# One attention pass for the first batch, a first chunk of 512 tokens, and a new split of the weight decode between ScalarE, VectorE and GpSimd

## The chip, the core and the metric

The kernel runs on one core of a Trainium2 chip. The core has five engines that each work through their own list of instructions in order: TensorE (PE in the profile; its weight loads are PEld), VectorE (DVE), ScalarE (ACT), GpSimd (POOL) and SyncE (SP), which here does nothing but issue the DMA transfers. The metric is the time of one execution in microseconds. The kernel before has a median of 1164.68 us over three runs, from 1161.99 to 1166.79.

## What is computed

A causal attention with a cumulative bias is followed by two gated feed-forward stages. Shapes: 4 batches, 8 heads, 576 positions, head size 64, so 2304 tokens of width 512; the first stage has 1536 hidden columns, the second 2048. The weights arrive as float64.

```python
scores = scale * np.matmul(q, k.transpose(0, 1, 3, 2))
cum = np.cumsum(np.maximum(s, 0.0), axis=-1)
bias = -(cum[:, :, :, None] - cum[:, :, None, :])
scores = np.where(causal, -1000000000.0, scores + np.minimum(bias, 0.0))
attn = np.exp(scores - np.max(scores, axis=-1, keepdims=True))
attn = attn / (np.sum(attn, axis=-1, keepdims=True) + 1e-09)
x = np.matmul(attn, v)           # heads side by side: 2304 x 512
x = (x @ w_a) * (x @ w_b) @ moe_w_out
h = x @ w_in
out = (np.maximum(h, 0.0) ** 2) @ moe2_w_out
```

## The kernel before

**Recording and planning.** Nothing is issued where it is written. Each operation is recorded with the engines that may do it and a cost for each. `Plan.order` (line 145) then goes through a simulated clock: for each engine it takes the operation that can start first, with a rank by stream (`RANK`, line 77) to choose between those that are ready, and so fixes both the engine and the place of every instruction. A buffer tag has a number of buffers; an operation that needs a new one waits until an older tile of the tag has had its last use. Costs are written by hand: `on_dve`, `on_act`, `on_gps` (lines 323 to 330) and `dma` (line 341), which counts 3.0 ns per kilobyte. Operations marked as using a port that VectorE and GpSimd share are kept apart in the plan. `copy` may go to ScalarE or VectorE, `subtract` to GpSimd or VectorE. Nearly every instruction carries line 246 in the profile, the line in `Plan.run` that issues it, so groups are told apart by tile names.

**Attention.** `attention` (line 723) works on pairs of heads. For a head, `softmax` (line 570) makes the scores (`st`) bank by bank: the products, then a product with a constant `mask` that adds the causal -1e9, then the row maximum on VectorE (`neg`), the exponential on ScalarE (`e`, with the row sum as a second output), a reciprocal (`one`) and the scaling of `e` by whichever of three engines is free. `weigh` (line 662) transposes `e` (`pt`), copies it (`ph`, and a remainder `pl`) and multiplies by the values (`av`), giving `u`. Batch 0 uses plain float32 operands (`fq`, `fk`, where the cumulative sum rides as a 65th row); batches 1 to 3 use split operands (high part and remainder) made by `prep` (line 531) from `raw` tiles.

**The first batch in two passes.** Before, batch 0 is done in a pass over queries 0 to 255 (stream "first", keys 0 to 255 alone) and later in a pass over queries 256 to 575 (stream "att").

**First stage.** `moe1` (line 852) goes over chunks of tokens: 256, 320, and four of 432. For each of 12 slices f of the hidden columns, 24 products of 128x128 weights with the chunk's columns make `ab` (two groups of 12), VectorE and ScalarE multiply and split the result, and after every third f 36 products `py` add to the output. A chunk is thus 432 products: 36 groups of 12. A chunk needs all heads of its tokens. Chunk 0 takes its input straight from `u`; others read it back from DRAM (`xd`).

**Weights.** `split_w` (line 815) decodes the three float64 matrices, 36 tiles of 128x512, on the chip: `decode` (line 780) loads 512 KB, scales the high word as a float and converts the low word with a scale (the two *scales*), shifts and merges the bits (two VectorE instructions), adds on GpSimd, casts to the high part `wh` on ScalarE and *subtracts* for the remainder (`wl`, `wlo`), which is also stored to DRAM (`wlab`, `wlo`) for the later chunks. The raw words land in `roomxh`, `roomxl` and, for the first `MORE` tiles, `words`. Chunk 0 runs f by f as the tiles appear. The second stage's weights are decoded the same way by `split2` (line 981) late in the first stage.

**Around the start.** `ssb`, `spos`, `ch`, `cl`, `maskf` and the q and k tiles of batches 1 to 3 share the tag `raw` (three buffers). `ch` and `cl`, the two parts of the cumulative sum, are stored to DRAM as `cd` when `operands` (line 492) is first called, which is in the preparation of batch 1. `maskf` is filled on GpSimd and cast to `mask` on ScalarE.

Of the kernel before, what the change touches and what calls it, by code (L numbers as in the profile page):

```python
# [7 lines left out]
F32 = mybir.dt.float32  # L8
# [8 lines left out]
P = 128  # L17
# [231 lines left out]
def attention_moe_moe(tc, q, k, v, s, w_a, w_b, w_out, w_in2, w_out2, out):  # L249
# [11 lines left out]
    CA = 256  # L261
    CB = S - CA
    GRP = 3
    GB = 4
    NT1 = 3
    CC = 432
# [6 lines left out]
    MORE = 24  # L273
# [49 lines left out]
    def on_dve(method, n, *args, two=False, each=1.04, **kw):  # L323
        return "DVE", 150 + each * n, two, method, args, kw
# [27 lines left out]
    def subtract(n, out, a, b, by="PD"):  # L352
# [10 lines left out]
        [scratch([NP, P, CB if b == 0 else S], F32, f"xd{b}")] for b in range(B)  # L363
    ]

    spans = [(0, CA), (CA, S)] + [(t, t + CC) for t in range(S, B * S, CC)]
# [14 lines left out]
    def blocks(q0, qn):  # L381

        if qn == S:
            return [(0, 64)] + [(64 + P * i, P) for i in range(4)], 0
        if q0 == 0:
            return [(0, P), (P, P)], 0
        return [(0, P), (P, P), (256, 64), (320, P), (448, P)], 2

    def load_values(b, p, q0, qn):

        t = at([P, NJ, P], F32, "val", 2, f"val{b}_{p}_{q0}")
        kb, _ = blocks(q0, qn)
# [20 lines left out]
    first_q = [at([P, S], F32, "T2q", 3, f"fq{i}") for i in range(3)]  # L413
    first_k = {}

    def load_first(hh, q0, qn):
        kn = q0 + qn
        tq = first_q[hh % 3]
        tk = first_k[hh, q0] = at([P, S], F32, "T2k", 3, f"fk{hh}_{q0}")
        dma(tk[:D, :kn].part("x"), k[0, hh, :, :kn], kn * 0.25)  # L420
        dma(tq[:D, :qn].part("x"), q[0, hh, :, q0 : q0 + qn], qn * 0.25)

    ssb = at([P, S], F32, "raw", 3, "ssb")[: B * H]
    dma(ssb, s.rearrange("b h s -> (b h) s"), 74)
    for hh in range(3):
        load_first(hh, 0, CA)

# [7 lines left out]
    spos = at([P, S], F32, "raw", 3, "spos")[: B * H]  # L435
# [5 lines left out]
    ch, cl = (at([P, S], F32R, "raw", 3, z)[: B * H] for z in ("ch", "cl"))  # L441
# [4 lines left out]
    maskf = at([P, S], F32, "raw", 3, "maskf")[:, :P]  # L446
# [8 lines left out]
    for i in range(4):  # L455
        t = [at_const([P, NJ + 2], F32, f"{z}{i}") for z in ("neg", "sum", "one")]
        for x in t:
            gps("memset", NJ + 2, x, 1.0)
        small.append(t)
# [3 lines left out]
    def score_banks(q0, qn):  # L463
        if qn == S:
            return [[(1, 0, 192), (2, 0, 320)], [(0, 0, 64), (3, 0, 448)], [(4, 0, 288)], [(4, 288, 288)]]
        if q0 == 0:
            return [[(0, 0, P), (1, 0, CA)]]
        return [[(2, 0, 320)], [(3, 0, 448)], [(4, 0, 288)], [(4, 288, 288)]]


    def weight_banks(q0, qn):
        if qn == S:
            return [(0, 320, [[0], [1, 2]]), (320, 256, [[1, 2], [3, 4], [0]])]
        if q0 == 0:
            return [(0, CA, [[0, 1]])]
        return [(256, 320, [[0, 4], [1], [3], [2]])]

    def load_pair(b, p, src, nm):
        t = at([P, S], F32, "raw", 3, f"raw{nm}")
        dma(t, src[b, 2 * p : 2 * p + 2].rearrange("h d s -> (h d) s"), 288)  # L480
        return t
# [26 lines left out]
    def prep_first(p, q0, qn):  # L508

        load_values(0, p, q0, qn)  # L510
        heads = []
        for hh in (2 * p, 2 * p + 1):
            if (hh, q0) not in first_k:
                load_first(hh, q0, qn)
            tk = first_k[hh, q0]
            dma(tk[D : D + 1, : q0 + qn].part("c"), cum[hh : hh + 1, : q0 + qn], 2)
            tq = first_q[hh % 3]
            scaled(qn, tq[:D, :qn].part("x"))
            heads.append((tq, tk))
        return heads  # L520
# [10 lines left out]
    def prep(b, p):  # L531
# [4 lines left out]
        load_values(b, p, 0, S)  # L536
        scaled(S, tq)
        heads = []
        for h in range(2):
            hh = b * H + 2 * p + h  # L540
            t1 = operands()
            t2q = at([P, S], F32R, "T2q", 3, f"t2q{nm}_{h}")
            t2k = at([P, S], F32R, "T2k", 3, f"t2k{nm}_{h}")
# [26 lines left out]
    def softmax(b, p, h, q0, qn, head):  # L570

        kb, first_block = blocks(q0, qn)
        banks = score_banks(q0, qn)
        nq = len(kb)
        nm = f"{b}_{p}_{q0}_{h}"
# [5 lines left out]
        for i, pieces in enumerate(banks):  # L581
            ps = mm_bank(f"st{nm}_{i}") if b == 0 and q0 == 0 and hh % 2 else bank(f"st{nm}_{i}")
# [5 lines left out]
            for blk, k0, kn in pieces:  # L588
                at_, m = kb[blk]
                qc = slice(at_ - q0, at_ - q0 + m)  # L590
# [44 lines left out]
            for blk, k0, m, to, kn, ee in held:  # L635
# [4 lines left out]
                    accum_out=tot[:m, c : c + 1].part(c), psum=True,  # L640
# [21 lines left out]
    def weigh(b, p, h, q0, qn, head, place, chunk, u):  # L662

        kb, first_block = blocks(q0, qn)
        g0, n, banks = chunk
        nm = f"{b}_{p}_{q0}_{h}_{g0}"
        parts = []
        for i, keys in enumerate(banks):
            ps = bank(f"pt{nm}_{i}", "t")
            calls, ins, off, spans = [], [ident], 0, []  # L670
            for j in keys:
                k0, m = kb[j]
                c0 = max(k0, g0)
                for blk in range(max(j, first_block), len(kb)):
# [434 lines left out]
```

## Time and profile before

The profiled execution is one of its own, outside the three runs.

| What | Value |
|---|---|
| median of three runs | 1164.68 us |
| profiled execution | 1163.58 us |
| its span, first to last instruction | 1161.8 us |
| granted TensorE clock, mean over the span | 0.964 |
| TensorE products | 5888 instructions recorded, 1105.1 us busy (95%) |
| VectorE | 1315 instructions, 670.9 us (58%) |
| ScalarE | 1164 instructions, 494.9 us (43%) |
| GpSimd | 284 instructions, 324.3 us (28%) |
| DMA | 143.85 MB, mean 124 GB/s |
| first and last product with chunk 0 | 46.2 and 239.7 us |
| first product of chunk 1 | 241.3 us |
| last product of batch 3's attention | 525.4 us |
| first product of the second stage | 752.0 us |

In the rows of the profile a tile's buffer number is left out: `ab<-xh,wh` is a product of a weight tile `wh` with a chunk's columns `xh`. Products overlap each other, so the time that one product is recorded with (350 ns for 432 columns) is longer than the time from one to the next; a group of 12 in the chain of waits gives the pace.

### The profile page before, as it was taken

The numbers are of one execution on the slowest core, as the hardware profiler recorded it, in microseconds if no ns is written. First come the engines' busy times: TensorE is split into PE (matmuls) and PEld (weight loads), VectorE is DVE, ScalarE is ACT, GpSimd is POOL, SyncE is SP. The second block draws the span as 40 slices with busy tenths as digits, with TensorE's granted clock in tenths as the row PEclk, the third lists the DMA queues.
The fourth block names the chain that finished last, engine by engine and source line by source line (L and its number), as shares of the span: only waits on it lengthen the run. The fifth ranks groups of instructions, "written<-read, shape, count | busy, mean of one in ns | idle before, by whom it ended". The sixth has DMA issues, their size and how long they took to land.

```text
span 1161.8 us, 16590 instructions
## 1 busy us (share of the span) xinstructions
PE 1105.1 (95%) x5888; PEld 969.6 (83%) x5888; DVE 670.9 (58%) x1315; ACT 494.9 (43%) x1164; POOL 324.3 (28%) x284
## 2 busy tenths in 40 slices
PE   5888987699999999999999999998999999999998
PEld 4666666599999999999999999987888888888887
DVE  6778988877888878863232257887232232232232
ACT  5567656557666665442121135455322222222222
POOL 3456655433433342210010036677100010000000
PEclk9689987799999999999999999999999999999999
DMA  6767575664456454335353387653020020010000
GB/s 186 221 187 237 184 219 156 192 175 149 151 170 178 137 158 116 115 100 154 113 164 124 101 271 239 195 175 124 1 73 1 1 73 1 1 55 1 1 37 19
DMA packets 91314, 143.85 MB, mean 124 GB/s; under 512 B 10320, under 2 KB 60240, under 8 KB 91232
## 3 DMA queue, kind: packets, MB, share of 16 engines
q1 hardware_dynamic: 91232, 142.80, 39.9%
q8 instruction: 46, 0.75, 0.3%
q14 instruction: 36, 0.29, 0.1%
HBM read 110.68 MB, written 23.22 MB: 115 GB/s over the span
## 4 chain that ended last, share of the span: by engine, by line
PE 83%; DVE 7%; DMA 5%; issue 1%; POOL 1%; ACT 1%; SPq 0%; DVEq 0%; POOLq 0%; ACTq 0%
PE ab L246 24%; PE po L246 16%; PE ph L246 16%; PE py L246 12%; PE st L246 6%; PE pt L246 5%; PE av L246 5%; DMA loo<-wlo 1%; DVE roomxl L246 1%; DVE neg L246 1%; DVE ph L246 1%; DMA lo<-wlab 1%; DVE one L246 1%; DMA roomxh<-in_moe_w_a 1%; DMA words<-in_moe_w_a 0%
## 5 line engine op out<-in xcount | busy, mean ns | idle before, releaser
L246 DVE SCALAR_TENSOR_TENSOR ph<-ph,r 128x512 f32<-128x512 f32 (+1 forms) x80 | 51.6, 645 | 198.7 <-ACT r L246 198.6
L246 ACT ACTIVATE r<-ph 128x512 f32<-128x512 f32 (+1 forms) x80 | 44.5, 556 | 221.5 <-PE ph L246 221.5
L246 PE MATMUL ab<-xh,wh 128*128 128x432 f32 (+1 forms) x384 | 134.4, 350 | 0.0
L246 PE MATMUL ab<-xl,wh 128*128 128x432 f32 (+1 forms) x384 | 132.7, 346 | 0.0
L246 PE MATMUL ab<-xh,lo 128*128 128x432 f32 (+1 forms) x384 | 132.7, 345 | 0.0
L246 PE MATMUL po<-w2h,g2h 128*128 128x512 f32 x288 | 113.0, 393 | 3.2 <-ACT g2h L246 3.1
L246 ACT ACTIVATE e<-st,neg 128x192 f32<-128x192 f32 (+4 forms) x192 | 92.3, 483 | 54.6 <-DVE neg L246 45.2
L246 PE MATMUL po<-w2l,g2h 128*128 128x512 f32 x288 | 113.0, 392 | 0.0
L246 PE MATMUL po<-w2h,g2l 128*128 128x512 f32 x288 | 112.7, 391 | 0.0
L246 DVE TENSOR_TENSOR ab<-ab,a 128x432 f32<-128x432 f32 (+2 forms) x72 | 40.7, 565 | 113.5 <-PE ab L246 109.4
L246 PE MATMUL pt<-ident,e 128*128 128x128 f32 (+3 forms) x480 | 89.3, 295 | 14.3 <-ACT e L246 5.7
L246 DVE TENSOR_REDUCE neg<-st 128x1 f32<-128x192 f32 (+4 forms) x192 | 79.0, 429 | 16.8 <-PE st L246 13.0
L246 PEld LDWEIGHTS pt<-ident,e 128*128 128x128 f32 (+3 forms) x480 | 57.0, 140 | 34.7 <-ACT e L246 7.6
L246 PE MATMUL py<-gh,wh 128*128 128x432 f32 (+1 forms) x240 | 85.0, 354 | 0.2 <-DVE gl L246 0.2
L246 PE MATMUL py<-gl,wh 128*128 128x432 f32 (+1 forms) x240 | 83.6, 348 | 0.0
L246 PE MATMUL py<-gh,loo 128*128 128x432 f32 (+1 forms) x240 | 83.5, 348 | 0.0
L246 DVE TENSOR_TENSOR g2l<-ph,g2h 128x512 fp32r<-128x512 f32 (+1 forms) x80 | 50.9, 638 | 44.1 <-ACT g2h L246 39.7
L246 ACT COPY a<-ab 128x432 f32<-128x432 f32 (+2 forms) x72 | 34.5, 480 | 93.2 <-PE ab L246 92.9
L246 PEld LDWEIGHTS ab<-xh,lo 128*128 128x128 f32 x384 | 72.2, 188 | 2.2
L246 PEld LDWEIGHTS ab<-xh,wh 128*128 128x128 f32 x384 | 72.4, 189 | 2.0
L246 PEld LDWEIGHTS ab<-xl,wh 128*128 128x128 f32 x384 | 72.4, 189 | 1.9
L246 PE MATMUL av<-ph,vs 128*128 128x320 f32 (+1 forms) x192 | 63.0, 330 | 5.6 <-DVE ph L246 4.7
(214 smaller groups left out, 2820.6 us busy)
## 6 DMA issues: line engine op xcount, KB each, us to landing
lo<-wlab SPq DMA_DIRECT2D x60, 512.0 KB
loo<-wlo SPq DMA_DIRECT2D x48, 384.0 KB
v_0r<-in_moe_w_in SPq DMA_DIRECT2D x16, 512.0 KB
v_1r<-in_moe_w_out SPq DMA_DIRECT2D x16, 512.0 KB
out<-o SPq DMA_DIRECT2D x18, 256.0 KB
roomxh<-in_moe_w_a SPq DMA_DIRECT2D x8, 512.0 KB
roomxh<-in_moe_w_b SPq DMA_DIRECT2D x8, 512.0 KB
roomxl<-in_moe_w_out SPq DMA_DIRECT2D x8, 512.0 KB
```

The costliest lines, as they stand in the source:

```text
L246: getattr(eng, method)(*map(real, args), **{k: real(a) for k, a in kw.items()})
```

## The change

Five things are changed together, and the planner then makes a new order of everything:

1. Batch 0's attention is one pass over all 576 queries, with the same banks as the other batches, all in stream "first". `FIRST` = 512 of its tokens go straight to chunk 0 (eight tiles `x0`), the last 64 to DRAM.
2. The chunks are 512 and four of 448, so five in place of six.
3. In `decode` both scales are done by ScalarE alone, for both stages' weights; the first stage's subtract is done by VectorE alone. The second stage's subtract stays on GpSimd.
4. Buffers are fewer: `raw`, `T2q`, `T2k` and `T1` have two in place of three, `ph` two in place of three, `MORE` is 20 in place of 24.
5. The planner counts 4.5 ns per kilobyte of DMA in place of 3.0, and counts VectorE's fast copies and scales as users of the port shared with GpSimd. The row sums get one reduction over three columns (two partial sums and 1e-9) in place of an addition of 1e-9 and, where there were two parts, a reduction of two.

```diff
-    CA = 256
-    CB = S - CA
+    FIRST = 512
-    NT1 = 3
-    CC = 432
+    NT1 = 2
+    CC = 448
-    MORE = 24
+    MORE = 20
...
-        return "DVE", 150 + each * n, two, method, args, kw
+        return "DVE", 150 + each * n, two or each < 1, method, args, kw
...
-        pl.call(("SP", kb * 3.0, False, "dma_start", (out, in_), {}), takes=takes, lag=lag)
+        pl.call(("SP", kb * 4.5, False, "dma_start", (out, in_), {}), takes=takes, lag=lag)
...
-    spans = [(0, CA), (CA, S)] + [(t, t + CC) for t in range(S, B * S, CC)]
+    spans = [(0, FIRST)] + [(t, t + CC) for t in range(FIRST, B * S, CC)]
...
-    ssb = at([P, S], F32, "raw", 3, "ssb")[: B * H]
+    ssb = at([P, S], F32, "raw", 2, "ssb")[: B * H]
...
-    maskf = at([P, S], F32, "raw", 3, "maskf")[:, :P]
+    maskf = at([P, S], F32, "raw", 2, "maskf")[:, :P]
...
-        if banks[-1][0][1]:
-            dve("tensor_reduce", 2, out=tot[:, nq - 1 : nq], in_=tot[:, nq - 1 : nq + 1], op=ALU.add, axis=AX.X)
-        qs = slice(first_block, nq)
-        dve("tensor_scalar_add", nq, one[:, qs], tot[:, qs], 1e-9)
+        qs = slice(0, nq)
+        dve(
+            "tensor_reduce", 3 * nq, out=one[:, qs], in_=tot[:, qs], op=ALU.add, axis=AX.X,
...
-        pl.call(
-            on_dve("tensor_scalar", n, hf, hf, 2.0**-112, None, op0=ALU.mult, each=0.52),
-            on_act("mul", n, hf, hf, 2.0**-112),
-        )
+        act("mul", n, hf, hf, 2.0**-112)
...
-        pl.call(
-            on_act("activation", n, low, low.bitcast(U32), AF.Copy, scale=2.0**-29),
-            on_dve("tensor_scalar", n, low, low.bitcast(U32), 2.0**-29, None, op0=ALU.mult, each=0.52),
-        )
+        act("activation", n, low, low.bitcast(U32), AF.Copy, scale=2.0**-29)
...
-                decode(w, i < 2, f, hi, lo, f"w{f}_{i}", words[k_ % len(words)], t, (), "PD")
+                decode(w, i < 2, f, hi, lo, f"w{f}_{i}", words[k_ % len(words)], t, (), "D")
...
-    trace("first", attention(0, 0, CA))
+    trace("first", attention(0))
...
-    trace("att", attention(0, CA, CB))
```

Three places of the new order matter below. On GpSimd, at the start of the program, before (`maskf` is the mask being filled, `neg0` and `sum0` are small constants, `e` the exponentials, `one` the reciprocals, and the last row is the add of the first decoded tile):

```order
L246 MEMSET fq2_94 1x576
L246 MEMSET maskf_113 128x128
L246 MEMSET neg0_117 128x7
L246 AFFINE_SELECT maskf_113<-maskf_113 128x128
L246 MEMSET sum0_123 128x7
...
L246 TENSOR_TENSOR e0_0_0_0_0_163<-e0_0_0_0_0_163,one0_127 128x128
L246 TENSOR_TENSOR e0_0_0_0_0_163<-e0_0_0_0_0_163,one0_127 128x256
...
L246 TENSOR_TENSOR roomxl_131<-roomxl_131,roomxh_115 128x512
```

and now, from the first add of a decoded tile on:

```order
L246 TENSOR_TENSOR roomxl_143<-roomxl_143,roomxh_132 128x512 x2
L246 TENSOR_TENSOR roomxl_143<-roomxl_143,words0_145 128x512
L246 TENSOR_TENSOR wt0_2_178<-wt0_2_178,roomxl_143 128x512
L246 TENSOR_TENSOR roomxl_143<-roomxl_143,words1_150 128x512
L246 TENSOR_TENSOR wt1_2_211<-wt1_2_211,roomxh_132 128x512
L246 TENSOR_TENSOR roomxl_143<-roomxl_143,roomxh_132 128x512
L246 TENSOR_TENSOR roomxl_143<-roomxl_143 128x512
L246 TENSOR_TENSOR roomxl_143<-roomxl_143,words1_150 128x512
L246 TENSOR_TENSOR wt2_2_253<-wt2_2_253,words0_145 128x512
L246 TENSOR_TENSOR roomxl_143<-roomxl_143,roomxh_132 128x512
L246 MEMSET maskf_295 128x128
L246 AFFINE_SELECT maskf_295<-maskf_295 128x128
```

The mask has moved from the head of the list to behind the adds of eleven decoded tiles. With two `raw` buffers `maskf` is the fifth tile of the tag and takes the buffer of `ch`, which is free once `ch` has been stored. That store, `cd<-ch`, now stands on SP behind fourteen loads of raw weights (`roomxh`, `roomxl`, `words`) and the stores of the first remainders:

```order
L246 DMA words1_150<-in_moe_w_a 128x4x256
L246 DMA roomxh_132<-in_moe_w_b 128x4x256
L246 DMA wlo0_206<-wl1_2_229 256x1x128 x2
L246 DMA wlab2_240<-wl2_0_234 128x512
L246 DMA roomxh_132<-in_moe_w_out 128x1024
L246 DMA roomxl_143<-in_moe_w_a 128x4x256
L246 DMA wlab2_240<-wl2_1_249 128x512
L246 DMA words1_150<-in_moe_w_out 128x1024
L246 DMA cd_267<-ch_115 32x576
L246 DMA words0_145<-in_moe_w_b 128x4x256
```

Each load among them waits until the buffer that it overwrites has been added. On TensorE, where the second chunk begins, before (`py0` is chunk 0's output, `st1_2_0` a score of batch 1's pair 2, `ab1_0` the second chunk's first product):

```order
L246 MATMUL py0_3_1_3_2482<-g0_11_2330,wh11_2_2308 128x256 x2
L246 MATMUL py0_3_1_3_2482<-g0_11_2330,loo0_3_1_2388 128x256
L246 MATMUL av1_1_0_1_0_2495<-ph1_1_0_1_0_0_2461,vs1_1_1_2183 128x320
...
L246 MATMUL st1_2_0_0_3_2519<-T11_1379 128x288
...
L246 MATMUL ab1_0_0_2525<-xh1_2379,wh0_0_320 128x320
```

and now:

```order
L246 MATMUL av2_0_0_320_3064<-ph2_0_0_320_2_3073,vs2_0_0_2811 128x256
L246 MATMUL st2_1_0_0_3089<-T10_968 128x320
...
L246 MATMUL st2_1_0_1_3100<-T10_968 128x448
...
L246 MATMUL pt2_0_1_0_0_3121<-ident_73,e2_0_1_1_3021 64x64
...
L246 MATMUL ab1_0_0_3133<-xh1_2623,wh0_0_158 128x448
```

The second chunk, which now holds tokens of batch 1, stands behind the whole of batch 1's attention and some of batch 2's; before it stood behind about four of batch 1's eight heads.

More of the change, by code (lines that the diff above doesn't have):

```diff
@@ L379, in at_const, with load_values @@
         return v
[L381 to L392, printed above, removed]
+    kb = [(0, 64)] + [(64 + P * i, P) for i in range(4)]
+    def load_values(b, p):
+        t = at([P, NJ, P], F32, *(("val", 1) if b else ("vs", 2)), f"val{b}_{p}")
         j = 0
@@ L440, in attention_moe_moe @@
         gps("memset", S, t[D : D + 1].part("c"), 1.0)
-    ch, cl = (at([P, S], F32R, "raw", 3, z)[: B * H] for z in ("ch", "cl"))
+    ch, cl = (at([P, S], F32R, "raw", 2, z)[: B * H] for z in ("ch", "cl"))
     act("copy", S, ch, cum)
@@ L455, in attention_moe_moe @@
     for i in range(4):
-        t = [at_const([P, NJ + 2], F32, f"{z}{i}") for z in ("neg", "sum", "one")]
-        for x in t:
+        t = [at_const([P, *n], F32, f"{z}{i}") for z, n in (("neg", [NJ + 2]), ("sum", [NJ, 3]), ("one", [NJ]))]
+        for x in t[::2]:
             gps("memset", NJ + 2, x, 1.0)
+        for c, x in ((0, 1.0), (1, 0.0), (2, 1e-9)):
+            gps("memset", NJ, t[1][:, :, c : c + 1], x)
         small.append(t)
[L463 to L476, printed above, removed]
+    banks = [[(1, 0, 192), (2, 0, 320)], [(0, 0, 64), (3, 0, 448)], [(4, 0, 288)], [(4, 288, 288)]]
+    weight_banks = [(0, 320, [[0], [1, 2]]), (320, 256, [[1, 2], [3, 4], [0]])]
     def load_pair(b, p, src, nm):
-        t = at([P, S], F32, "raw", 3, f"raw{nm}")
+        t = at([P, S], F32, "raw", 2, f"raw{nm}")
         dma(t, src[b, 2 * p : 2 * p + 2].rearrange("h d s -> (h d) s"), 288)
@@ L506, in operands, with prep_first @@
         return T1[i % NT1]
-    def prep_first(p, q0, qn):
-        load_values(0, p, q0, qn)
+    def prep_first(p):
+        load_values(0, p)
         heads = []
         for hh in (2 * p, 2 * p + 1):
[L513 to L518, printed above, removed]
+            if hh not in first_k:
+                load_first(hh)
+            tk = first_k[hh]
+            dma(tk[D : D + 1].part("c"), cum[hh : hh + 1], 2)
+            tq = first_q[hh % 2]
+            scaled(S, tq[:D].part("x"))
             heads.append((tq, tk))
@@ L660, in softmax, with weigh @@
         return place
[L662 to L666, printed above, removed]
+    def weigh(b, p, h, head, place, chunk, u):
+        g0, n, key_banks = chunk
+        nm = f"{b}_{p}_{h}_{g0}"
         parts = []
-        for i, keys in enumerate(banks):
+        for i, keys in enumerate(key_banks):
             ps = bank(f"pt{nm}_{i}", "t")
@@ L673, in weigh @@
                 c0 = max(k0, g0)
-                for blk in range(max(j, first_block), len(kb)):
+                for blk in range(j, len(kb)):
                     at_, mq = kb[blk]
@@ L721, in weigh, with first_x, attention @@
         )
-    def attention(b, q0=0, qn=S):
+    first = [[at([P, FIRST], F32R, "x0", 2 * ND, f"x0{z}_{d}") for d in range(ND)] for z in range(2)]
+    def first_x(d, o, n):
+        return [t[d][:, o : o + n] for t in first]
+    def attention(b):
         steps = []
@@ L754, in attention @@
         return steps
-    first = [
-        [sb([P, W], F32R, t, GB, f"first{t}{z}")[:, : 2 * CA].rearrange("p (d c) -> p d c", d=2) for z in range(HD)]
-        for t in ("gh", "gl")
-    ]
-    def first_x(d, o, n):
-        return [t[d // 2][:, d % 2, o : o + n].part(d % 2) for t in first]
     def new_x(nm, second=False):
```

77 lines of the change are left out of this document (36 added, 41 removed).

## The prediction

> **What bounds the kernel now.** I read the slices of the span first, then four stages, then the chain of waits inside them. In the slices each digit is the busy share of a fortieth of the span in tenths; PEclk is the granted clock.
>
> ```profile
> PE   5888987699999999999999999998999999999998
> DVE  6778988877888878863232257887232232232232
> PEclk9689987799999999999999999999999999999999
> ```
>
> The first eight slices are unlike the rest: TensorE has gaps and a clock below full, and VectorE is at its busiest. The stages, cut at the first product of chunk 1, the end of attention and the start of the second stage of weights, show busy time and in brackets the instructions; the last columns are granted clock, DMA share and GB/s.
>
> ```profile
> core 0: us, PE busy (x) PEld busy (x) DVE busy (x) ACT busy (x) POOL busy (x), PEclk, DMA share, GB/s
> 0.00:241.30 241.30, 193.31 (x991) 148.90 (x991) 194.83 (x403) 141.98 (x361) 122.52 (x119) 0.84 0.64 195
> 241.30:525.40 284.10, 282.52 (x1886) 266.89 (x1886) 227.50 (x534) 168.95 (x468) 92.55 (x85) 1.00 0.49 145
> 525.40:751.70 226.30, 226.06 (x1155) 216.94 (x1154) 100.04 (x154) 65.06 (x120) 51.75 (x39) 1.00 0.54 171
> 751.70:1161.80 410.10, 403.18 (x1863) 336.83 (x1861) 148.48 (x225) 118.86 (x217) 57.47 (x42) 1.00 0.13 41
> ```
>
> From 241.3 us on TensorE is never without work for more than a few us and runs at clock 1.00: 920.5 us in which only a smaller amount of product work can save time. Before that VectorE is busy 194.8 of 241.3 us. So the time is the moment at which TensorE becomes full, plus the product work left then.
>
> **Term 1: product work.** The chain gives the pace of 12 products with 256, 320, 432 and 512 columns (start, length, what):
>
> ```profile
> 130.97 1.44 PE ab L246 x12
> ...
> 311.73 1.81 PE ab L246 x12
> ...
> 399.82 2.36 PE ab L246 x12
> ...
> 854.20 2.72 PE ph L246 x12
> ```
>
> A chunk is 36 such groups: 51.8, 65.2, 85.0 and 97.9 us. 448 columns are not in the trace; between 432 and 512 lies 2.43, which is 87.5 us a chunk (bounds 85.0 and 97.9; the nearer one is 432). Before: 51.8 + 65.2 + 4 x 85.0 = 457.0. After: 97.9 + 4 x 87.5 = 447.9. Fewer groups save only 9 us.
>
> What is left at the first product of the second chunk: before, 920.5 us. Of this the five chunks were 65.2 + 340.0 = 405.2, and will be 350.0: 55.2 less. In the second stage of the table, chunks 1 and 2 and 105 products of chunk 3 take 65.2 + 85.0 + 20.7 = 170.9 of 284.1 us, which leaves 113.2 for 20 heads, 5.66 a head. By the orders, the new point stands 5.6 heads later (scores and weighing counted apart): 31.7 less. So 920.5 - 55.2 - 31.7 = 833.6 us are left after it. **If the second chunk starts at 328.2 us, nothing changes; each us earlier is a us won.**
>
> **Term 2: when the second chunk starts.** Three stretches.
>
> *Until the mask.* Before, the mask was cast at 6.95 us and the first score product began at 7.92, held by the cumulative sum alone:
>
> ```profile
> 6.95 0.28 ACT L246 CAST mask<-maskf 128x128 bf16<-128x128 f32 x1
> ...
> 7.92 1.62 PE L246 MATMUL st<-fk,fq 65*128 65x128 f32 x4 [7.92 <-DMA fk<-cum]
> ...
> 10.00:48.00 38.00, 30.95 (x117) 22.14 (x116) 28.55 (x73) 22.25 (x66) 16.15 (x17) 0.78 0.71 218
> ```
>
> Now the mask waits for `cd<-ch`, and all of TensorE waits with it, for its first bank needs the mask; so do the row maxima on VectorE and the exponentials on ScalarE. Ahead on SP stand about 1.6 MB of attention operands, 14 raw loads of 0.524 MB and 8 stores of 0.262 MB: 11.0 MB. At the last row's 218 GB/s, with 0.8 MB in the first 10 us, they have landed at 57 us. The store itself only needs the tenth tile decoded: 8.1 MB, 44 us, and some 3 us of scale, shift, merge and add. Bounds 47 and 57; I take **52**. VectorE does thirteen decodes' first half meanwhile, so the stretch is not lost to it.
>
> *Batch 0's attention, up to chunk 0's first result.* I gave every instruction of both orders the mean of its row (a new size the mean of a row of that size) and added them up to the first `ab1_0`: VectorE 217.8 before, 263.5 now; ScalarE 165.6 and 246.0. Records overlap, so 217.8 was 194.8 busy (0.894) and 165.6 was 142.0 (0.857). The parts, for VectorE: 25 scales go, -19.8; 28 subtracts come, +25.3; one pass in place of two, -9.1; chunk 0 twice as wide, +13.3; 5.6 more later heads with their preparation, +34.2; the rest +1.7. For ScalarE: 25 scales +16.9; batch 0 +4.2; chunk 0 +4.9; later heads +45.3; rest +9. The rows behind the edits:
>
> ```profile
> L246 DVE TENSOR_SCALAR roomxh<-roomxh 128x512 f32<-128x512 f32 x8 | 8.2, 1027 | 0.9 <-DMA roomxh<-in_moe_w_a 0.9
> L246 ACT ACTIVATE roomxh<-roomxh 128x512 f32<-128x512 f32 x8 | 5.4, 679 | 1.4 <-DMA roomxh<-in_moe_w_a 0.8 <-DMA roomxh<-in_moe_w_b 0.6
> L246 DVE TENSOR_TENSOR wl<-roomxl,wh 128x512 fp32r<-128x512 f32 x7 | 6.7, 955 | 0.0
> L246 POOL TENSOR_TENSOR wl<-roomxl,wh 128x512 fp32r<-128x512 f32 x17 | 22.7, 1335 | 16.8 <-ACT wh L246 13.4 <-DVE roomxl L246 1.9 <-DVE wlo L246 1.2
> L246 DVE TENSOR_TENSOR ab<-ab,a 128x256 f32<-128x256 f32 x12 | 5.2, 430 | 5.8 <-PE ab L246 4.8 <-ACT e L246 0.9
> L246 DVE SCALAR_TENSOR_TENSOR ph<-ph,r 128x512 f32<-128x512 f32 x64 | 44.7, 698 | 172.7 <-ACT r L246 172.7
> ```
>
> In this stretch VectorE has 80.6 us of instructions, 72.1 busy; ScalarE 83.9, 72. With little but attention to do VectorE was busy 28.55 of 38 us (0.751, the row 10 to 48). At that share: **96** us. At the 0.842 of the whole time from 48 to 241.3 it would be 86.
>
> *Chunk 0 with batch 1.* VectorE 151.5, 135.4 busy; at 0.842, 161 us. TensorE needs 97.9 for chunk 0 and 9.3 x 5.66 = 53 for heads, 151. Both above 0.84 at once is more than the stage 241.3 to 525.4 shows (VectorE 227.5 of 284.1, 0.80), so I take **166** (bounds 151, TensorE alone, and 178, a tenth above 161).
>
> GpSimd loses 28 subtracts of 1335 ns, 37 of its 122.5 us; it ends no long wait that the start's chain shows, so I count nothing for it.
>
> A rule on this: the row of a shift, `roomxl<-roomxh`, and the same shift into `wt` differ only in what runs beside them.
>
> ```profile
> L246 DVE TENSOR_SCALAR roomxl<-roomxh 128x512 int32<-128x512 int32 x16 | 11.0, 689 | 0.6 <-issue 0.6
> L246 DVE TENSOR_SCALAR wt<-roomxl 128x512 int32<-128x512 int32 x5 | 2.1, 426 | 0.1
> ```
>
> The Trainium skill, page "SBUF — State Buffer", section "SBUF: two separate sides", says that VectorE and GpSimd hold a shared pair of ports one at a time, for a whole instruction. With 30% less of GpSimd, some 108 shifts, merges and subtracts would lose 30% of 0.26 us each, 8 us by my estimate, and the sum below would be about 10 us lower.
>
> **The sum.** 52 + 96 + 166 = 314; 314 + 833.6 = 1147.6 of span; the profiled execution is 1.8 us longer than its span, and the median 1.1 us above that execution: 1150.5, rounded to **1150**, 1.3% faster. The later edits (ScalarE's scales in `split2`, one reduction for the row sums) lie beside a full TensorE, with ScalarE at 118.9 of 410 us: nothing. If that cover were gone, 18 scales of 0.68 us would be 12 us.
>
> **Rivals.**
>
> *ScalarE becomes the bound: slower.* After the mask it has 246.0 - 28.2 = 217.8 us of instructions, 186.6 busy, up to the second chunk. My sum asks a share of 0.71 of it. Its highest share so far:
>
> ```profile
> 148.00:198.00 50.00, 38.90 (x214) 31.54 (x214) 43.81 (x90) 32.59 (x83) 29.14 (x24) 0.77 0.65 199
> 350.00:400.00 50.00, 49.38 (x320) 46.32 (x319) 41.25 (x99) 33.73 (x94) 16.28 (x14) 1.00 0.56 159
> ACT e L246 <- DVE neg L246: 25.1, 22, 3.4
> ```
>
> At the 0.65 of the start: 287 us, the second chunk at 339, 1176. It decides from a share of 0.676 down, just what 350 to 400 shows. Against it: ScalarE was not the limit there; its longest wait up to 241 us, the last row, was for VectorE's row maxima.
>
> *The clock takes it back: no change.* In the second stretch TensorE has batch 0 alone, at most 8 x 5.66 = 45 us of work in 96. At half clock that is 90, and at the share of the row 10 to 48 (30.95 of 38) 111 us: +15, 1165. For it: that row's clock of 0.78, and 0.77 from 148 to 198. Against: 45 us of work can also wait without delaying VectorE. The Trainium skill, "TensorE: Matmul & The Clock Gate", Part 1, says that an idle window of some 3.4 us halves the clock; by it the whole stretch could run at half. The clocks above fit.
>
> *The order fits the chip better: more is won.* The old plan counted transfers as faster than they are, and the chain holds waits for them:
>
> ```profile
> 182.10 6.14 DMA roomxh<-in_moe_w_a
> ...
> 226.32 6.92 DMA loo<-wlo
> ```
>
> If they go: mask at 47, attention at 0.842 in 86, then TensorE's 151 plus a little, 285 in all, 1121.
>
> **How the numbers follow.** Forecast 0.40, better order 0.18, clock 0.20, ScalarE 0.17, and 0.05 for a longer wait for the mask with any of them. Half a percent, about what a measurement of this kernel can tell from no change, is 1158.9 to 1170.5. Faster 0.58, same 0.20, slower 0.22. The range goes from the better order (1122) to just past the ScalarE case (1180).
>
> **What would show it.** Right: the first score product ends and the first row maximum begins at about 52 us, with eleven to thirteen decoded tiles ahead; the first `ab` near 148; chunk 1 near 314; from there TensorE without gaps and 834 us to the end, groups of 12 at 2.43. Wrong: a first maximum past 57, ScalarE the busier engine between 52 and 314 with VectorE waiting for `e`, a clock of 0.5 through batch 0's attention, gaps of TensorE after the second chunk's start, or a second chunk past 328.

## The result and the profile after

The changed kernel takes 1147.1 us (median of 4 runs, 1146.08 to 1147.98), the kernel before 1164.73 us beside it: a ratio of 0.985 with a 95% interval from 0.9828 to 0.9872, so 1.3 to 1.7% faster. The forecast was 1150. The profiled execution took 1146.95 us with a span of 1145.0, where the forecast's sum had a span of 1147.6. That is close, but two errors of 17 and 14 us cancel in it.

The slices of the span after, read as those of before:

```profile
PE   0399899999899999999999999969999999999998
DVE  5767687788788777743322346666232232232232
PEclk9999999999899999999999999988999999999999
```

TensorE does almost nothing in the first slice and little in the second, is then nearly full, and has one hole later (the 6). The clock row is at or near full from the mask on, but its first digits are too high, as the last section shows. The stages, cut at the mask, the first `ab` of chunk 0, the first `ab` of the second chunk, and the first product of the second stage (busy time, instructions in brackets, granted clock, DMA share, GB/s):

```profile
0.00:45.20 45.20, 2.05 (x4) 1.17 (x4) 30.90 (x39) 25.90 (x45) 18.74 (x41) 1.00 0.83 264
45.20:138.40 93.20, 86.53 (x397) 57.68 (x398) 61.68 (x154) 65.42 (x186) 24.40 (x22) 0.96 0.43 127
138.40:297.20 158.80, 155.15 (x866) 130.79 (x866) 133.47 (x282) 115.80 (x284) 72.05 (x61) 0.99 0.58 176
297.20:723.90 426.70, 425.80 (x2350) 392.00 (x2349) 240.60 (x483) 192.95 (x462) 96.87 (x85) 1.00 0.48 147
723.90:1145.00 421.10, 403.14 (x1862) 336.98 (x1860) 149.08 (x221) 131.36 (x240) 59.28 (x44) 0.98 0.13 43
```

The columns of busy time are TensorE, its weight loads, VectorE, ScalarE and GpSimd. Before, the whole start up to 241.3 us ran at a clock of 0.84. Now the view gives 0.96 and 0.99 for the two stretches after the mask, and TensorE is busy 0.93 and 0.98 of them. The mask came as the orders had said (rows of SP, GpSimd, ScalarE and TensorE in the timeline; the bracket is the idle time before):

```profile
38.51 0.42 SPq L246 DMA_DIRECT2D cd<-ch  x1
...
43.40 0.21 POOL L246 MEMSET maskf<- 128x128 f32 x1 [1.30 <-DMA cd<-ch]
...
44.90 0.29 ACT L246 CAST mask<-maskf 128x128 bf16<-128x128 f32 x1
...
45.24 0.39 PE L246 MATMUL st<-identb,mask 128*128 128x128 bf16 x2 [35.20 <-ACT mask L246]
```

The hole, in the chain of waits (start, length, what; after 758.8 us TensorE is no longer in it):

```profile
756.06 2.73 PE ph L246 x12
...
771.60 0.66 ACT v_1r L246
...
775.03 0.59 ACT g2h L246
...
775.66 4.37 PE po L246 x11
```

and in TensorE's waits from 297 us on, with the same wait in the kernel before behind it (total, times, longest):

```profile
PE po L246 <- ACT g2h L246: 14.2, 1, 14.2
```

```profile
PE po L246 <- ACT g2h L246: 3.1, 1, 3.1
```

ScalarE casts `g2h`, the input of the next `po`, only after it has scaled and cast several tiles of second-stage weights.

| | forecast | measured |
|---|---|---|
| mask | 52 (47 to 57) | 45.2 |
| batch 0's attention, to the first `ab` | 96 | 93.2 |
| chunk 0 with batch 1, to the second chunk | 166 (151 to 178) | 158.8 |
| second chunk starts | 314 | 297.2 |
| from there to the end | 833.6 | 847.8 |

### The profile page after: what moved, and what is told of

Read it like the earlier page. It is cut to its first block, busy times and chain, and to the rows that moved or that the text cites. A ratio compares the mean times of both kernels' runs of the same rounds, so it can differ in the third digit from the quotient of the medians.

```text
span 1145.0 us, 15537 instructions
## 1 busy us (share of the span) xinstructions
PE 1072.7 (94%) x5472; PEld 918.6 (80%) x5472; DVE 615.7 (54%) x1176; ACT 531.4 (46%) x1214; POOL 271.3 (24%) x251
## 4 chain that ended last, share of the span: by engine, by line
PE 92%; DVE 3%; ACT 2%; DMA 1%; SPq 1%; issue 1%; POOL 0%; ACTq 0%; DVEq 0%; POOLq 0%
PE ab L246 26%; PE po L246 17%; PE ph L246 17%; PE py L246 13%; PE st L246 7%; PE av L246 6%; PE pt L246 5%; DMA words<-in_moe_w_a 1%; SPq L246 1%; DVE v_1t L246 1%; DVE roomxl L246 1%; ACT e L246 1%; DMA words<-in_moe_w_out 0%; DVE wt L246 0%; DVE wl L246 0%
## 5 line engine op out<-in xcount | busy, mean ns | idle before, releaser
L246 PE MATMUL po<-w2h,g2h 128*128 128x512 f32 x288 | 113.2, 393 | 14.2 <-ACT g2h L246 14.2
L246 PE MATMUL ab<-xh,wh 128*128 128x448 f32 x288 | 107.3, 373 | 0.0
L246 ACT ACTIVATE e<-st,neg 128x192 f32<-128x192 f32 (+2 forms) x192 | 91.1, 478 | 32.1 <-DVE neg L246 28.7
L246 PE MATMUL ab<-xh,lo 128*128 128x448 f32 x288 | 105.9, 368 | 0.0
L246 PE MATMUL ab<-xl,wh 128*128 128x448 f32 x288 | 105.9, 368 | 0.0
L246 PE MATMUL py<-gh,wh 128*128 128x448 f32 (+1 forms) x240 | 90.4, 377 | 0.0
L246 PE MATMUL py<-gh,loo 128*128 128x448 f32 (+1 forms) x240 | 89.0, 371 | 0.0
L246 PE MATMUL py<-gl,wh 128*128 128x448 f32 (+1 forms) x240 | 88.9, 370 | 0.0
L246 PE MATMUL pt<-ident,e 128*128 128x128 f32 (+2 forms) x480 | 83.1, 285 | 5.4 <-ACT e L246 2.8
L246 DVE TENSOR_REDUCE neg<-st 128x1 f32<-128x192 f32 (+2 forms) x192 | 75.9, 423 | 21.5 <-PE st L246 19.9
L246 PE MATMUL ph<-yhy,w2l 128*128 128x512 f32 (+1 forms) x192 | 67.9, 354 | 0.0
```

The source lines that it names most:

```text
L246: getattr(eng, method)(*map(real, args), **{k: real(a) for k, a in kw.items()})
```

## The experiments

Each kernel was timed beside the kernel before on the same chip. Its ratio is to that kernel, whose median was 1165.09 us in the first group of four, 1164.85 in the second and 1163.75 in the third. Any edit makes the planner write a new order, so a run shows an edit with the order that it brings.

**First group: the mask, the scales, the decode.**

*mask_early.* The two stores of the cumulative sum are recorded right behind the sum.

```diff
     dve("tensor_tensor", S, out=cl, in0=cum, in1=ch.bitcast(F32), op=ALU.subtract, two=True)
+    dma(cd[:, 0, :].part(0), ch.bitcast(F32), 74)
+    dma(cd[:, 1, :].part(1), cl.bitcast(F32), 74)
...
-        if i == 0:
-            dma(cd[:, 0, :].part(0), ch.bitcast(F32), 74)
-            dma(cd[:, 1, :].part(1), cl.bitcast(F32), 74)
```

> The changed kernel, with the two stores of the cumulative sum recorded straight behind the sum and not with the preparation of batch 1, so that the buffer of the mask is free at about 10 us. Theory A, the 35.2 us for which TensorE waits for the mask are lost: from 45.2 us on TensorE is busy 86.5 of 93.2 and 155.4 of 159.0 us, so it can't make them up, and an earlier start is won as far as VectorE allows (226.3 us of VectorE up to the second chunk, at the share 0.84 that it has in the second stretch, is 269 us): second chunk at about 270 us, time about 1120 us. Theory B, the wait is covered: the decode work done in it (30.9 us of VectorE, 25.9 of ScalarE in 45.2) must then be done beside the attention: second chunk within 5 us of 297, time 1142 to 1152 us.

Measured: 1156.28 us, 0.9927 (0.9904 to 0.9949), so the wait of 35 us removed makes the kernel 9 us slower (the next kernel, on the same chip, has the late mask and takes 1147.06). Both theories fell. The mask is there at 11.1 us and the first `ab` comes 35 us earlier, at 103.0, yet the second chunk starts at 307.4, 10 us later. Windows from the first `ab` to the last product of chunk 0, and from there to the second chunk, the changed kernel first:

```profile
138.40:281.80 143.40, 143.40 (x794) 120.97 (x793) 121.09 (x251) 105.63 (x254) 62.41 (x52) 1.00 0.58 175
281.80:297.20 15.40, 11.75 (x75) 9.82 (x74) 12.37 (x31) 10.17 (x31) 9.63 (x10) 0.89 0.64 181
```

```profile
103.00:247.30 144.30, 134.05 (x647) 108.89 (x647) 116.77 (x221) 98.00 (x214) 61.90 (x48) 0.95 0.70 215
247.30:307.40 60.10, 49.11 (x231) 40.19 (x229) 43.62 (x105) 36.80 (x104) 21.91 (x22) 0.63 0.37 106
```

Chunk 0 itself takes the same time, but with the early mask it is through 60 us before the second chunk may start (15 in the changed kernel). In these 60 us TensorE has the attention that the second chunk needs and no dense work beside it: 231 products at a clock of 0.63, with short waits for VectorE and ScalarE. The tile view of the first operand `T` of the later batches' scores (count, durations, first and last start) shows when that attention began, the changed kernel first:

```profile
L246 PE MATMUL st<-T x144: 192/312/548, 128.6 to 487.2; 66*128 66x288 f32 x48, 66*128 66x320 f32 x24, 66*128 66x192 f32 x24, 66*128 66x448 f32 x24
```

```profile
L246 PE MATMUL st<-T x144: 193/313/743, 153.6 to 501.1; 66*128 66x288 f32 x48, 66*128 66x320 f32 x24, 66*128 66x192 f32 x24, 66*128 66x448 f32 x24
```

With the early mask only 9 of 36 tiles are decoded (counted by ScalarE's casts `wh`) when chunk 0 begins, and VectorE and ScalarE then spend 103 to 145 us on decode and chunk 0, with no exponential in between: none starts from 92.6 to 156.2 us, where the changed kernel's longest gap of that kind before the second chunk is 12.2 us. With the late mask it is 20 tiles, and batch 1 begins 25 us earlier, before chunk 0.

*Theory C*, formed from this and named in the expectations below: the wait for the mask is a head start for the decode. There it is worded as late weights starving TensorE beside chunk 0. The windows above suggest a closer wording: the head start lets batch 1 begin early enough to run beside chunk 0, and without it TensorE is left with attention alone, and throttled.

*late_scales.* In `decode`, the second stage's two scales may go to either engine again.

```diff
-        act("mul", n, hf, hf, 2.0**-112)
+        if by == "P":
+            pl.call(
+                on_dve("tensor_scalar", n, hf, hf, 2.0**-112, None, op0=ALU.mult, each=0.52),
+                on_act("mul", n, hf, hf, 2.0**-112),
+            )
+        else:
+            act("mul", n, hf, hf, 2.0**-112)
...
```

> The changed kernel, with the two scales of the second stage's weights free to go to ScalarE or VectorE, as in the kernel before; the first stage's stay on ScalarE alone. Theory A, the 14.2 us for which TensorE waits at 761 us for a cast (3.1 us in the kernel before) come from ScalarE's list, in which the scales and the casts of one tile stand one behind the other and each waits for VectorE or GpSimd: the gap falls to 3 to 5 us, time about 1136 us. Theory B, the gap comes from the plan's other constants or from the shorter last chunks, which leave less time before the second stage: the gap stays above 10 us, time 1145 to 1149 us.

Measured: 1147.06 us, 0.9839 (0.9804 to 0.9875), and the gap is 14.2 us as it was. The planner moved only 4 of the 64 scales to VectorE (18 were there before the change), so this is a weak test of the scales. Theory B's numbers came out: the gap stays, and freeing the scales brings nothing here.

*old_decode.* The decode of the kernel before, both scales and the subtract.

```diff
-        act("mul", n, hf, hf, 2.0**-112)
+        pl.call(
+            on_dve("tensor_scalar", n, hf, hf, 2.0**-112, None, op0=ALU.mult, each=0.52),
+            on_act("mul", n, hf, hf, 2.0**-112),
+        )
...
-                decode(w, i < 2, f, hi, lo, f"w{f}_{i}", words[k_ % len(words)], t, (), "D")
+                decode(w, i < 2, f, hi, lo, f"w{f}_{i}", words[k_ % len(words)], t, (), "PD")
```

> The changed kernel, with the decode of both stages as in the kernel before: scales on ScalarE or VectorE, the first stage's subtract on GpSimd or VectorE. The prediction's account: up to the second chunk VectorE gets 25 scales back (19.8 us) and loses 28 subtracts (25.3 us), ScalarE loses 16.9 us, so the start is no later, second chunk at 285 to 300 us, and the gap at 761 us falls to about 3: time 1125 to 1140 us. Rival: GpSimd with 28 more subtracts slows VectorE's shifts and merges and stands later itself, the second chunk moves past 305 us and eats the gain: time 1147 us or more.

Measured: 1152.02 us, 0.9888 (0.9844 to 0.9933); second chunk at 301.9, gap 14.2. The prediction's account fell: undoing the decode's change costs 4.7 us at the start, and the gap stays. The rival's time came true, its second chunk past 305 did not. With the choice free again, the planner gave GpSimd 16 of the 36 subtracts (28 in the kernel before) and VectorE 17 of the first stage's scales (25) and 4 of the second's (18), so the old decode came back in part only.

*before_decode.* The same edit the other way round, made to the kernel before.

> The kernel before, with only the change of the decode: scales on ScalarE alone, first subtract on VectorE alone. The prediction's account: VectorE 5.5 us more and ScalarE 16.9 us more in a start that VectorE sets: 1160 to 1172 us. Rival, the decode is where the gain comes from: 1145 to 1155 us.

Measured: 1151.56 us, 0.9875 (0.9838 to 0.9913), so 13.5 us of gain from an edit that the prediction had as a small load on the start. Which half of it does this was left to the third group.

**Second group: the gap and theory C.**

*early6.*

```diff
-    EARLY = 10
+    EARLY = 6
```

> The changed kernel, with only the number of second-stage slices that are recorded ahead of the second stage cut from 10 to 6. Theory A: the 14.2 us gap is a turn in a ring of buffers. The cast g2h takes its buffer from the tag gh, whose turns go by the order of recording, and a remainder tile of slice 13 is recorded ahead of it in that tag, so the cast can't be issued before that tile's decode has begun; recorded later, the tile stands behind it: the gap falls below 3 us, time 1132 to 1137 us. Theory B: the second stage simply eats a slice in 5.4 us and the decode makes one in 8 to 10, so TensorE waits for weights instead: waits of 10 us or more in all between 724 and 800 us, time 1144 us or more.

Measured: 1131.69 us, 0.9747 (0.9703 to 0.979). The gap is gone: from the second chunk to the end TensorE has one wait,

```profile
PE av L246 <- DVE ph L246: 0.9, 1, 0.9
```

and this part takes 1127.6 - 296.2 = 831.4 us. ScalarE's order around the cast shows the turn. In the changed kernel it stands behind the tiles of slice 12 and with those of 13 (`v13_1` is the tile whose remainder takes a buffer of the cast's tag):

```
L246 CAST g2h0_3_7753<-ph0_3_7711 128x512
...
L246 CAST w2h12_0_7893<-v12_0t_7879 128x512
L246 CAST g2h0_4_7898<-ph0_4_7755 128x512
L246 CAST g2h0_5_7902<-ph0_5_7801 128x512
...
L246 ACTIVATE v12_1r_7871<-v12_1r_7871 128x512
L246 ACTIVATE v13_0r_7883<-v13_0r_7883 128x512
```

With 6, the casts `g2h0_4` and `g2h0_5` follow `g2h0_3` by 6 and 11 rows, and the first row of slice 13 stands 22 rows behind the second of them. The gap fell as theory A had it, and the time is at the edge of its range. The second stage does not outrun its weights, so theory B fell.

*dma3* and *port_old* each undo one of the two planning constants.

```diff
-        pl.call(("SP", kb * 4.5, False, "dma_start", (out, in_), {}), takes=takes, lag=lag)
+        pl.call(("SP", kb * 3.0, False, "dma_start", (out, in_), {}), takes=takes, lag=lag)
```

> The changed kernel, with 3.0 ns per kilobyte of DMA in the plan in place of 4.5. By the new order the mask stands behind the adds of 2 decoded tiles in place of 11, so it is cast at 18 to 25 us and not at 45. Theory C, the wait for the mask is a head start for the decode: with less of it TensorE starves and is throttled in the first chunk, the granted clock from the first ab to the second chunk is below 0.93 (0.99 in the changed kernel, 0.86 with the early mask), second chunk at 300 to 308 us, time 1148 to 1156 us. Theory A of the early mask, the wait is lost time: second chunk at 270 to 280 us, time below 1130 us. The gap at 761 us stays above 8 us.

Measured: 1151.03 us, 0.9889 (0.9868 to 0.991), second chunk at 303.9, gap 9.4.

```diff
-        return "DVE", 150 + each * n, two or each < 1, method, args, kw
+        return "DVE", 150 + each * n, two, method, args, kw
```

> The changed kernel, without the new rule by which VectorE's fast copies and scales are planned as users of the shared port. By the new order the mask stands behind the adds of 22 decoded tiles, twice as many as in the changed kernel: cast at 75 to 90 us. Theory C, the head start pays only until the decode is no longer what TensorE waits for; what is beyond that is lost, since batch 0 and the first chunk can't take less than TensorE's 70 and 154 us: second chunk at 310 to 330 us at a clock of 0.98 or more, time 1155 to 1175 us. Rival, the decode sets the end of the start whatever the order: second chunk at 295 to 303 us, time 1142 to 1150 us.

Measured: 1165.13 us, 1.0 (0.9985 to 1.0015), mask at 76.9, second chunk at 324.6, gap 9.3. Their two stretches:

```profile
22.30:122.10 99.80, 90.39 (x380) 58.54 (x380) 65.99 (x162) 66.37 (x180) 22.06 (x19) 0.91 0.43 133
122.10:303.90 181.80, 165.58 (x864) 137.09 (x863) 151.22 (x303) 127.79 (x307) 73.59 (x61) 0.93 0.58 180
```

```profile
76.90:169.70 92.80, 86.37 (x418) 58.37 (x419) 63.89 (x159) 57.70 (x174) 28.80 (x28) 0.98 0.30 89
169.70:324.60 154.90, 154.46 (x867) 130.67 (x867) 124.63 (x269) 101.64 (x256) 63.35 (x53) 0.99 0.47 144
```

The first is *dma3*, with the mask behind 2 adds, the second *port_old*, behind 22. Both came out in theory C's numbers, the clock of *dma3* at the edge of its bound (0.93): with too little head start the clock falls; with too much the stretch is at its floor (TensorE busy 154.5 of 154.9) and the rest of the wait is lost.

*old_all.* Old decode and both old constants together; the one pass, the chunks, the buffers and the row sums stay.

> The changed kernel with the old decode and the old constants of the plan together, so that what is left is the one pass, the chunks, the buffers and the row sums; the mask stands behind 3 adds. Theory C: the mask at 20 to 28 us, clock below 0.92 in the first chunk, GpSimd with 28 subtracts more, second chunk at 305 to 315 us, the gap of the second stage below 5 us: time 1143 to 1155 us. Rival, the one pass and the chunks bring nothing and the gain lies in the decode and the plan: 1160 us or more.

Measured: 1140.1 us (1136.89 to 1145.82), 0.9799 (0.9765 to 0.9832): below theory C's range, and its start missed too, with the second chunk at 299.2 and not past 305, at a clock of 0.93. Mask at 20.8, behind two adds and a subtract, largest wait of TensorE after it 0.9 us, 835.9 us left. Beside *old_decode*, whose edit differs in the constants alone, this shows what the constants do, with the order that they bring (GpSimd has 25 subtracts here, 16 there): the second chunk is 2.7 us earlier without them, and the rest 12.3 us shorter, nearly the gap.

**Third group: less decode, the halves of the decode's change, a middle mask.**

*early_light.* The early mask, and in the first stage the low word's scale and its add are left out; the weights then keep only the high word's bits.

```diff
-        act("activation", n, low, low.bitcast(U32), AF.Copy, scale=2.0**-29)
-        gps("tensor_tensor", n, out=t, in0=t, in1=low, op=ALU.add)
+        if by == "P":
+            act("activation", n, low, low.bitcast(U32), AF.Copy, scale=2.0**-29)
+            gps("tensor_tensor", n, out=t, in0=t, in1=low, op=ALU.add)
```

> The kernel with the early mask, with less decode in the first stage: the scale of the low word (ScalarE, 0.67 us a tile) and its add (GpSimd, 1.37 us a tile) are left out, so the weights keep only the bits of the high word; products, DMAs and everything else are as in the early mask. Theory C, it is the decode standing beside attention and the first chunk that starves TensorE: with some 24 us less of ScalarE and 49 us less of GpSimd the stretch from the first ab to the second chunk falls from 204 us to 160 to 180 us and the granted clock in it rises from 0.86 to 0.93 or more, time 1120 to 1135 us. Rival, the attention of batch 1 beside the first chunk does it, whatever the decode: stretch above 195 us, clock below 0.89, time above 1147 us.

Measured: 1147.75 us, 0.9854 (0.982 to 0.9889), second chunk at 298.0.

```profile
11.20:112.80 101.60, 90.53 (x381) 59.17 (x381) 70.48 (x174) 67.81 (x184) 5.66 (x7) 0.90 0.58 180
112.80:298.00 185.20, 171.03 (x877) 141.23 (x876) 147.76 (x305) 114.32 (x285) 48.06 (x44) 0.92 0.55 172
```

Between the two: less decode shortens the stretch by 19 of the 46 us and the clock rises to 0.92, but neither reaches what theory C asked. Chunk 0 is through at 251.2 here, 46.8 us before the second chunk, so the tail of attention alone is still there. Batch 1's first score comes at 127.8, as in the changed kernel (128.6), and the second chunk at 298.0 and 297.2: with the same start of batch 1, a mask 34 us earlier and a first chunk that ends 31 us earlier bring nothing. That speaks for the wording with batch 1 and against the one with late weights.

*before_sub* and *before_scales*, each made to the kernel before: the first changes `"PD"` to `"D"` in `split_w` alone, the second puts the two scales on ScalarE alone.

> The kernel before, with only the first stage's subtract on VectorE alone. Theory D, the gain of the decode's change (13.5 us on the kernel before) comes from GpSimd, which loses 28 subtracts (37 us): its part of the gain is most of it, 1150 to 1157 us. Theory E, it comes from VectorE, which loses 25 scales that took 0.8 us each: the subtract alone puts 25 us on VectorE and is no gain, 1163 to 1175 us.

> The kernel before, with only the scales of both stages on ScalarE alone. Theory D: little, 1160 to 1166 us. Theory E: all or more of the gain, 1140 to 1153 us.

Measured: the subtract alone 1147.4 us, 0.9862 (0.9809 to 0.9915); the scales alone 1167.55 us, 1.0028 (1.0002 to 1.0053). So the whole gain comes with taking 28 subtracts of 1.3 us from GpSimd, though VectorE takes them over at some 0.8 us each. Theory D had this right, and both runs lie just beyond its ranges. How it comes about is less clear. In GpSimd's waits up to the second chunk, the kernel before has:

```profile
POOL wl L246 <- ACT wh L246: 13.9, 9, 3.4
...
POOL wlo L246 <- ACT wh L246: 7.7, 4, 4.4
```

A subtract needs the cast of its tile from ScalarE. While GpSimd's list stood at it, 21.6 us in all, no add behind it was made, and each tile needs one. But without the subtracts GpSimd waits longer at the adds: up to the second chunk it is idle 241.3 - 122.5 = 118.8 us before and 214.9 - 93.0 = 121.9 in *before_sub*, whose row (the order of columns as above, GpSimd the fifth) is

```profile
0.00:214.90 214.90, 175.19 (x899) 132.59 (x899) 168.44 (x365) 131.40 (x327) 93.04 (x96) 0.84 0.67 210
```

So GpSimd does not wait less; it has 29.5 us less to do, and the second chunk starts 26.4 us earlier, in part because 92 products fewer stand ahead of it. The last cast `wh` starts at 187.8 us in place of 220.5. That the subtracts also slow VectorE counts for little: the shifts and merges of 16 of the 36 tiles, the kernel before ahead of *before_sub* (the shift of before stands in the prediction at 689 ns),

```profile
L246 DVE SCALAR_TENSOR_TENSOR roomxl<-roomxh,roomxl 128x512 int32<-128x512 int32 x16 | 13.8, 871 | 0.1
```

```profile
L246 DVE SCALAR_TENSOR_TENSOR roomxl<-roomxh,roomxl 128x512 int32<-128x512 int32 x16 | 13.3, 834 | 0.0
L246 DVE TENSOR_SCALAR roomxl<-roomxh 128x512 int32<-128x512 int32 x16 | 8.2, 511 | 0.0
```

went from 24.8 to 21.5 us. Over all 36 tiles the two instructions take 52.0 us in the kernel before, 49.1 in *before_sub* and 43.5 in *before_decode*; the run that saves most there gains no more time than the other.

*early6_dma42.* *early6*, with the mask between those of *dma3* and the changed kernel.

```diff
-    EARLY = 10
+    EARLY = 6
...
-        pl.call(("SP", kb * 4.5, False, "dma_start", (out, in_), {}), takes=takes, lag=lag)
+        pl.call(("SP", kb * 4.2, False, "dma_start", (out, in_), {}), takes=takes, lag=lag)
```

> The kernel with 6 slices recorded ahead, and 4.2 ns per kilobyte of DMA in the plan in place of 4.5: the mask stands behind 5 adds in place of 11, and is cast at 27 to 35 us. Theory C, by the lengths measured from the first ab to the second chunk (204, 182, 159, 155 us with the mask at 11, 22, 45, 77 us) about 172 us at 30 us: second chunk at 294 to 302 us, clock 0.94 to 0.98, time 1128 to 1138 us, no different from the 1131.7 with the mask at 46 us by more than 5 us. Rival, the wait is lost time: second chunk at 282 us or before, time 1118 us or less.

Measured: 1129.18 us, 0.9698 (0.9664 to 0.9733), second chunk at 296.9: theory C. Its interval overlaps with that of *early6*, so the two are not told apart. Both beat the changed kernel; they are the versions to keep.

```profile
28.40:124.20 95.80, 86.85 (x380) 56.70 (x380) 65.39 (x157) 63.99 (x178) 22.59 (x21) 0.93 0.41 128
124.20:296.90 172.70, 162.32 (x877) 135.35 (x876) 147.76 (x295) 126.96 (x309) 81.52 (x69) 0.97 0.61 185
```

The mask put together, for the kernels with the new decode whole (us; "tail" is from the last product of chunk 0 to the second chunk):

| kernel | adds ahead of the mask | mask cast | tiles decoded at the first `ab` | batch 1's first score | second chunk | tail | clock from first `ab` to second chunk |
|---|---|---|---|---|---|---|---|
| mask_early | 0 | 11.1 | 9 | 153.6 | 307.4 | 60.1 | 0.86 |
| dma3 | 2 | 22.3 | 14 | 144.1 | 303.9 | 49.1 | 0.93 |
| early6_dma42 | 5 | 28.4 | 14 | 143.4 | 296.9 | 33.8 | 0.97 |
| the changed kernel | 11 | 45.2 | 20 | 128.6 | 297.2 | 15.4 | 0.99 |
| port_old | 22 | 76.9 | 26 | 149.0 | 324.6 | 0.3 | 0.99 |

From batch 1's first score to the second chunk it takes 154 to 176 us in all five (170 in *early_light*, 162 in *old_all*). A later mask, up to 45 us, does not make that attention later, and fills the tail. At 77 us it does (149.0 against 128.6), and the wait is lost.

## Why the prediction was right, and where only its sum was

**Right: the product work.** Groups of 448 columns take 2.43 us, as interpolated, where nothing stands between them:

```profile
319.39 2.43 PE ab L246 x12
```

The 833.6 us left after the second chunk's start became 831.4 once the gap was away (*early6*), 835.9 in *old_all*.

**Wrong: "The later edits ... lie beside a full TensorE ...: nothing."** This term was mis-sized: the second stage has a gap of 14.2 us where it had 3.1. The prediction's price for a lost cover (12 us, for ScalarE's scales) has the size but not the cause. The gap stays with the old decode as far as that came back, shrinks to 9.4 or 9.3 without one constant of the plan, and is gone without both (with the old decode) or when four slices fewer are recorded ahead. It is a turn in a ring of buffers, which go round in the order of recording; the constants had pushed that turn behind a slow decode.

**Right, early by 6.8 us: the mask.** The chain (buffer, store, loads ahead on SP, eleven adds) is there word for word. The size missed its bounds of 47 to 57: the loads ran at 264 GB/s in this stretch, not at the 218 taken from 10 to 48 us of the kernel before. At 264, the 11.0 MB take 41.7 us, and the store landed at 43.4.

**Right in size, wrong in its reason: batch 0's attention.** 96 was 72.1 us of VectorE at a share of 0.751; it is 61.7 us at 0.66 of the 93.2. TensorE is busy 86.5 of them, so "at most 8 x 5.66 = 45 us of work" was wrong: that was the price of a later batch's head. For the first 20 us TensorE ran at about half speed (last section), but after that it is still busy 68.7 of 72.7 us, so batch 0's heads cost more in any case:

```profile
65.70:138.40 72.70, 68.69 (x346) 46.95 (x345) 49.30 (x121) 54.64 (x154) 20.28 (x19) 0.95 0.36 103
```

That the size came out is luck.

**Half right: chunk 0 with batch 1.** 158.8, within its bounds and nearer the lower one, "TensorE alone", 151. VectorE came out as forecast (133.5 us against 135.4, share 0.84), but TensorE, at 0.98, set the length. That VectorE sets the start by its sum is contradicted by *before_sub*: 28 subtracts more for VectorE, 16 us less for the kernel.

**Wrong: GpSimd at nothing.** "it ends no long wait that the start's chain shows" was true and not enough. The subtract alone is worth 16 us on the kernel before, though on the changed kernel undoing the decode edit, which came back in part only, costs only about 5 (*old_decode*). That the head start has taken the pressure off there is likely, not shown. The sum by the Trainium skill's rule in "SBUF — State Buffer", section "SBUF: two separate sides", pointed the right way. Its path, faster shifts and merges, is there in size in *before_decode* (8.5 us, where that sum had 8) but is not what wins: *before_sub* saves only 2.9 us on them and gains as much time.

**The rivals.** ScalarE had the share that the sum asked, 181.2 of 252.0 us (0.72 against 0.71), and was no bound. The clock did take something back: in the first 20 us of batch 0, where the rival had it, without making that stretch longer than forecast, and in the tail after chunk 0, where it had not, most of all when the mask is early. The rule that this rival named, of the Trainium skill's "TensorE: Matmul & The Clock Gate", Part 1, is borne out by the gap of the second stage. TensorE is idle from 761.5 us on, the clock is halved from 765.4, and stays so for 3.5 us after work resumes.

```profile
761.50:765.40 3.90, 0.00 (x0) 0.00 (x0) 3.28 (x5) 3.01 (x6) 2.18 (x3) 1.00 0.31 115
765.40:775.60 10.20, 0.00 (x0) 0.00 (x0) 8.07 (x6) 4.97 (x10) 8.02 (x7) 0.50 0.50 154
775.60:779.10 3.50, 3.44 (x8) 2.72 (x9) 3.11 (x5) 2.68 (x6) 2.18 (x2) 0.50 0.43 139
779.10:785.00 5.90, 5.90 (x27) 4.86 (x27) 3.27 (x3) 2.96 (x6) 5.00 (x4) 1.00 0.58 176
```

**The mask as a cost.** The prediction added the wait and set VectorE's work in it against it. The runs show a trade that comes out even or better up to some 45 us. *old_all* shows that the pass, the chunks, the buffers and the row sums together bring 24.8 us, of which the plan's constants gave back about 12 and the new decode brought about 5 again; the whole change brings 17.6.

**Open.** What holds batch 1's attention at 154 to 176 us, and how much of the tail is the clock's and how much the chain's, was not separated: no run kept TensorE busy with idle work there. How much of GpSimd's part is its list and how much its time was not tried. Which of the one pass, the five chunks, the fewer buffers and the new row sums brings the 24.8 us was not tried either; no run undoes one of them alone. With every edit the order changed too.

## What to carry to other kernels

An engine that waits at the start need not lose that time if the others use it for work that would later stand in the way; before counting a removed wait as a gain, ask which dense work then runs out first. Here 35 us less of waiting made the kernel 9 us slower. Ask of an engine off the chain not only how busy it is, but which later work needs something that stands far down its list. When a late gap keeps its length whatever is done to the work around it, look for an order of buffers, not for a slow engine.

## What was not expected of the hardware

With the early mask the clock stays at half for one stretch of 44.4 us, although TensorE is busy 0.87 of it and none of its waits there is longer than 1.7 us:

```profile
259.90:304.30 44.40, 38.53 (x157) 31.73 (x158) 30.68 (x72) 25.00 (x70) 14.22 (x15) 0.50 0.26 75
```

```profile
PE av L246 <- DVE ph L246: 3.4, 4, 1.7
```

So in this run short products with short waits were enough to keep it there.

The clock that the profile prints is not always the one that ran. The trace of the changed kernel has its first clock record at 65.7 us, and the views print 1.00 for what lies before it. But the four products of one bank take 2.21 us up to 49.74 us, and 1.18 us once the records have begun:

```profile
45.43 2.21 PE L246 MATMUL st<-fk,fq 65*128 65x448 f32 x4
...
49.74 2.21 PE L246 MATMUL st<-fk,fq 65*128 65x448 f32 x4
...
66.91 1.18 PE L246 MATMUL st<-fk,fq 65*128 65x448 f32 x4
```

TensorE came out of the wait of 35.2 us at about half speed and stayed there for some 20 us, of which it was busy 17.8, the first 11 without a gap. So the 0.96 of batch 0's stretch is too high. The kernel before has its first record at 21.2 us, so its 0.84 of the start is a little too high as well. In every run of the table the first record lies ahead of the first `ab`, so its last column is not touched by this.

In the changed kernel's timeline, VectorE's merge takes 1.65 us when a GpSimd add is running as it starts, and 0.68 at 44.82 us, where GpSimd has nothing to do:

```profile
38.78 1.34 POOL L246 TENSOR_TENSOR wt<-wt,words 128x512 int32<-128x512 int32 x1 [0.68 <-DVE wt L246]
39.02 1.65 DVE L246 SCALAR_TENSOR_TENSOR roomxl<-roomxh,roomxl 128x512 int32<-128x512 int32 x1
...
44.82 0.68 DVE L246 SCALAR_TENSOR_TENSOR roomxl<-roomxl 128x512 int32<-128x512 int32 x1
```

The add ends at 40.12 and the merge 0.55 us later, as if most of it had come after the add.
